# A long convolution and a cosine-gated layer: the last transform step with its data as weights, and x turned in blocks

## The chip, the cores and the metric

The kernel runs on one core of one Trainium2 chip, in one launch, in float32 throughout. The core has a matrix engine (TensorE, here PE, with PEld for its weight loads), a vector engine (DVE), a scalar engine (ACT), GpSimd (POOL), and SyncE (SP), which here does nothing but issue DMAs. The metric is the device time of one execution in microseconds; a kernel is judged by the median of its runs.

## What is computed

Four sequences of 12480 positions and 128 channels pass through a causal convolution and then through a layer with a cosine gate. Cut to what matters:

```python
h_filt = np.maximum(pos_emb @ w1, 0.0) @ w2 * window      # (12480, 128), one filter per channel
u = x * v                                                 # (4, 12480, 128)
y = irfft(rfft(u, 2 * S) * rfft(h_filt, 2 * S))[:, :S]    # convolution over the positions
tokens = (x * y).reshape(49920, 128)
h = tokens @ w_in                                         # 128 -> 2048
out = (h * np.cos(h)) @ w_out                             # 2048 -> 128
```

## The kernel before

The convolution is made as a Fourier transform of length 11520 = 96 x 120 that is written as matmuls. A position is a pair (n1, n2): n1 counts 104 rows of 120 positions, n2 the place in a row. For each of the four batches there are four steps, each a generator that emits its instructions a bit at a time.

- `f1_units`: 64 steps, one per pair of channels. `f1_mm` (L407) takes a slice of the buffer `slots` as weights (104 rows, 124 columns) against the table `c1`; ACT or DVE bring the result back into `slots` (`f1_evict`).
- `f2_units`: 48 steps, one per pair of frequencies. `f2_mm` (L448) has a table `w` as weights and moves `slots`; DVE and POOL multiply by the filter's transform `h` (L471 to L474).
- `i1_units`: 64 steps, one per pair of channels. `i1_mm` (L479) takes `slots` as weights (120 rows, 96 columns); ACT and DVE bring the result back (L487, L489).
- `i2_units`: 30 groups of four n2. `i2_mm` (L504) has a table `t` as weights (96 rows, 104 columns, from `tm`, which batch 0 makes and the others load from `td`) and moves 128 channels from `slots`; eight matmuls make one PSUM bank of 104 rows (n1) by 4 x 128. `i2_out` multiplies it by `xs`, the same rows of x, on DVE (L511) and stores the product `zs` in the DRAM buffer `zd`.

The one buffer `slots` has 128 partitions and, in each, 64 pairs of channels by 240 places by the 2 channels of a pair. So one channel over all places lies 8 bytes apart, and all channels of one place lie in pairs 1920 bytes apart. During `i2_units` of a batch, `u_units` of the next one loads x and v (L376), multiplies them (L395) and writes their sums into `slots` (L401).

The layers work in 97 tiles of up to 512 tokens: 4 n2 by up to 128 rows of `zd`. `moe_load` fetches a tile as `zb`, with the tokens on the partitions (L727); `moe_turn` turns it by four transposes on PE (L126 with `zb`) and a copy on ACT (L737), to have the channels on the partitions (`at`). Then come 16 steps: `moe_up` (L743, then ACT L746, DVE L749, POOL L752), `moe_act` (ACT L757, DVE L759) and, four steps later, `moe_down` (L768). `moe_back` turns the result by four more transposes (L126 with `ot`), and `moe_store` writes it out in one to three DMAs (L794).

The order is written out by hand and is the same on every run: each engine works through its own list in that order, and so does SyncE with its DMAs. The main loop goes through the layers' steps, and after each it lets the convolution's generators run for an amount of work that they state themselves:

```python
            owed += 1.0
            while owed > 0.0:
                owed -= next(conv, owed)
```

One group of `i2_units` counts 3.5 layer steps in batch 0, 3 in batches 1 and 2, and 1.5 in batch 3, which has no next batch beside it. `load(n)` first lets the convolution run until the rows of tile n have been made, so the layers start after the first group, and once batch 3 is through they are alone. In `i2_units` the loads for a group are issued one group ahead (`before`), in batch 3 two ahead.

Every DMA is issued by SyncE. The DMAs take eight semaphores in turn, so each waits until the one eight places before it has landed.

Of the kernel before, what the change touches and what calls it, by code (L numbers as in the profile page):

```python
# [30 lines left out]
def kernel(  # L31
# [74 lines left out]
    LAG = 4  # L106
    WCOL = 256

    dram = ctx.enter_context(tc.tile_pool(name="dram", bufs=1, space=DRAM))
    hd = dram.tile([N1 // 2, N2, 2, CB, 4], F32, name="hd")  # L110
    zd = dram.tile([NROWS, G, D], F32, name="zd")
# [241 lines left out]
    def filter_out(pool, bank, aT, slots, j, w2_sb):  # L353

        ps = bank()
        for i, jj in enumerate((j, H - 1 - j)):
            nc.tensor.matmul(ps[0:FR, i * 2 * D:(i + 1) * 2 * D], aT[:, jj, 0:FR],
                             w2_sb[:, :], start=True, stop=True)
        above = pool.tile([FR, 2, CB, 2], F32, name="above", bufs=2)
        pj = ps[0:FR, :].rearrange("p (n b i) -> p n b i", n=4, i=2)  # L360
        nc.scalar.copy(out=above[:, :, :, :], in_=pj[:, 2:4])
        a = H - 2 - 2 * j
        for place, op in ((a, ALU.add), (ODD + a, ALU.subtract)):
            nc.vector.tensor_tensor(
                slots[0:FR, :, place:place + 2, :].transpose([0, 2, 1, 3]),
                pj[:, 1::-1], above[:, :, :, :], op=op)
# [14 lines left out]
    def clear_gap(u):  # L381

        nc.gpsimd.memset(u[:, :, H:ODD, :], 0.0)
# [13 lines left out]
    def u_sums(u, tiles, a):  # L397
        both = tiles[0][:, :, :].rearrange("p h (n b i) -> p h n b i", n=UA, i=2)
        below, above = both[:, 0, ::-1, :, :], both[:, 1, :, :, :]
        for place, op, e in ((a, ALU.add, nc.gpsimd), (ODD + a, ALU.subtract, nc.vector)):  # L400
            e.tensor_tensor(u[0:R, :, place:place + UA, :].transpose([0, 2, 1, 3]),  # L401
                            below, above, op=op)


    def f1_mm(ps, u, b, i):

        nc.tensor.matmul(ps[0:KE, i * 2 * N1:(i + 1) * 2 * N1], u[:, b, 0:KE, i],  # L407
                         c1[0:u.shape[0], :, :].rearrange("p r k -> p (r k)"),
                         start=True, stop=True)
# [10 lines left out]
    def f1_evict(ps, b, share):  # L420
        copy, negated = f1_takers(b, share)
        pj = ps[:, 0:4 * N1].rearrange("p (i r k) -> p r k i", i=2, r=2)
        copy(out=parts[0:ODD, :, :, b, :], in_=pj[0:ODD])
        yield
        copy(out=parts[ODD:KE, 0, :, b, :], in_=pj[ODD:KE, 1])
        negated(parts[ODD:KE, 1, :, b, :], pj[ODD:KE, 0])
        yield

    def f1_evict_filter(ps, b, share):

        copy, negated = f1_takers(b, share)
        pj = ps[:, 0:4 * N1].rearrange("p (i k) -> p k i", i=2)
        near, far = ftile[:, b, :, :], above[:, b, :, :]
        copy(out=near[0:ODD], in_=pj[0:ODD, 0:N1 + KF])
        copy(out=far[0:ODD], in_=pj[0:ODD, N1 + KF:])
        yield
        copy(out=near[ODD:KE, 0:N1], in_=pj[ODD:KE, N1:])
        negated(near[ODD:KE, N1:], pj[ODD:KE, 0:KF])
        negated(far[ODD:KE], pj[ODD:KE, KF:N1])
        yield  # L440

    def f2_mm(ps, w, k1, i, filt=False):


        k = k1 + i
        pi = ps[0:N2, :].rearrange("p (r b g i) -> p g r b i", r=2, g=2, i=2)[:, i]
        if not filt:
            nc.tensor.matmul(pi, w[:, i, :], parts[0:KE, :, k], start=True, stop=True)  # L448
        elif k < KF:
            both = ftile[0:KE, :, k:k + N1 + 1:N1, :].rearrange("p b r i -> p r b i")  # L450
            nc.tensor.matmul(pi, w[:, i, :], both, start=True, stop=True)
        else:
            for r, src in enumerate((ftile[0:KE, :, k, :], above[0:KE, :, k - KF, :])):
                nc.tensor.matmul(pi[:, r], w[:, i, :], src, start=True, stop=True)

    def f2_product(pool, ps, h, k1, whole):


        y = parts[0:N2, :, k1:k1 + 2, :, :].rearrange("p r k b i -> p r b (k i)")
        t = pool.tile([N2, 2, CB, 4], F32, name="t", bufs=1 + whole)  # L460
        uu = ps[0:N2, :].rearrange("p (r b j) -> p r b j", r=2, j=4)
        if whole:
            for r, (dst, hh) in enumerate(((y, h[:, :, :, :]), (t[:, :, :, :], h[:, ::-1, :, :]))):
                u = uu[:, r]
                twice = bass.AP(tensor=u.tensor, offset=u.offset,
                                ap=[u.ap[0], [0, 2], *u.ap[1:]])
                nc.vector.tensor_tensor(dst, twice, hh, op=ALU.mult)  # L467
                yield
# [8 lines left out]
    def i1_mm(ps, b, i):  # L477
        for r in range(2):
            nc.tensor.matmul(  # L479
                ps[0:N1, (i * 2 + r) * N2:(i * 2 + r + 1) * N2],  # L480
                parts[0:N2, r, :, b, i],
                cs[:, r, :], start=True, stop=True)

    def i1_evict(pool, ps, b):
# [3 lines left out]
        for h, op in ((0, ALU.add), (1, ALU.subtract)):  # L488
            nc.vector.tensor_tensor(slots[0:N1, b, h * N2:(h + 1) * N2, :], pj[:, 0],  # L489
                                    other[:, :, :], op=op)  # L490
            yield

    def i2_mm(ps, t, g, part):
        for i in range(part * G // 2, (part + 1) * G // 2):
# [8 lines left out]
            for r, place in enumerate(places):  # L503
                nc.tensor.matmul(ps[0:R, i * D:(i + 1) * D], t[:, i, r, :],  # L504
                                 slots[0:N1, :, place, :], start=(r == 0), stop=(r == 1))

    def i2_out(pool, ps, xs, b, g):
        if b == 0:
            yield
        zs = pool.tile([R, 2, UA, D], F32, name="zs")  # L510
        nc.vector.tensor_tensor(  # L511
            zs[:, :, :, :].rearrange("p h n d -> p (h n d)"), ps[0:R, :],
            xs[:, :, :].rearrange("p h n -> p (h n)"), op=ALU.mult)
        z = zs[:, :, :, :].rearrange("p h n d -> p (h n) d")
        row = (b * NG + g) * R
        if row > 0:
            nc.sync.dma_start(zd[row:row + R, :, :], z)
        else:
            zbs[0] = z
        made[0] += 1  # L520
        yield

    rows_psum = []
    made = [0]
    zbs = {}
# [65 lines left out]
    def f2_units(bank):  # L591
        with tc.tile_pool(name="there", bufs=3) as pool:
            ws, hs = {}, {}

            def before(j):
                ws[j] = pool.tile([KE, 2, N2], F32, name="w")
                nc.sync.dma_start(ws[j][:, :, :], wd[j, :, :, :])
                hs[j] = pool.tile([N2, 2, CB, 4], F32, name="h")
                nc.sync.dma_start(hs[j][:, :, :, :], hd[j, :, :, :, :])
# [10 lines left out]
    def f2_both_units(bank):  # L610

        with tc.tile_pool(name="both", bufs=2) as pool:
# [15 lines left out]
            def after(j, ps):  # L628
                h = pool.tile([N2, 2, CB, 4], F32, name="h", bufs=3)
                nc.scalar.activation(h[:, :, :, :].rearrange("p r b j -> p (r b j)"),  # L630
                                     ps[1][0:N2, :], AF.Copy, scale=1.0 / M)
                nc.sync.dma_start(hd[j, :, :, :, :], h[:, :, :, :])
# [32 lines left out]
    def i2_units(bank, b, bufs):  # L665

        with tc.tile_pool(name="back", bufs=2, side="left" if b else "right") as pool:
            ts, xss = {}, {}

            def before(j):  # L670
                ts[j] = pool.tile([N1, G, 2, R], F32, name="tm", bufs=bufs)
                xss[j] = pool.tile([R, 2, UA * D], F32, name="xs", bufs=bufs)
                load_pairs(xss[j], x, b, n2s(j)[0], n2s(j)[UA])
                if b == 0 and j not in SOME:
                    return make_group(pool, j, ts[j], 1)
                nc.sync.dma_start(ts[j][:, :, :, :], td[j, :, :, :, :])

            def mm(j, ps, i):
                if i == 0:
                    ps = bank()  # L680
                i2_mm(ps, ts[j], j, i)
# [3 lines left out]
                             lambda j, ps: i2_out(pool, ps, xss.pop(j), b, j),  # L685
                             4 if b == 0 else 2, ahead=bufs - 1, skip=int(b == 0))

    def inverse_units(bank, b):
# [6 lines left out]
        new = u_units(b + 1, 3, slots[0:R, :, :, :],  # L695
# [10 lines left out]
    def forward_units(bank, back):  # L706
# [3 lines left out]
        yield from f1_units(bank, slots[0:R, :, :, :])  # L710
# [13 lines left out]
    def moe_load(pool, n):  # L724
        m, row = rows_of(n), first_row(n)
        zb = pool.tile([P, G, D], F32, name="zb", bufs=2)
        nc.sync.dma_start(zb[0:m, :, :], zd[row:row + m, :, :])  # L727
        zbs[n] = zb

    def moe_turn(pool, n):  # L730
        m = rows_of(n)
        zb = zbs.pop(n)
        pt = ps_h.tile([P, BANK], F32, name="ph")
        for i in range(G):
            transpose(pt[:, i * m:(i + 1) * m], zb[0:m, i, :], ident)
        at = pool.tile([D, BANK], F32, name="at")
        nc.scalar.copy(out=at[:, 0:G * m], in_=pt[:, 0:G * m])  # L737
# [62 lines left out]
    with tc.manual_schedule():  # L800
        with tc.tile_pool(name="psum", bufs=8, space=PSUM) as psum, \
# [5 lines left out]
            slots = spool.tile([P, CB, 2 * N2, 2], F32, name="slots")  # L807
            parts = slots[:, :, 0:2 * N1, :].rearrange("p b (r k) i -> p r k b i", r=2)
            above = slots[:, :, 2 * N1:2 * N2, :]
            aT = above.rearrange("p b j i -> p b (j i)")  # L810
# [5 lines left out]
            with tc.tile_pool(name="layers", bufs=1, side="right") as pool:  # L816
# [10 lines left out]
                first_u = u_units(0, 3, slots[0:R, :, :, :],  # L827
# [24 lines left out]
            ftile = fpool.tile([P, CB, N1 + KF, 2], F32, name="ftile")  # L852
            clear_gap(ftile[0:FR, :, :, :])
# [5 lines left out]
            f1 = f1_units(bank, ftile[0:FR, :, :, :], 0.53, f1_evict_filter)  # L859
# [27 lines left out]
            beside(f1_units(bank, slots[0:R, :, :, :], 0.55),  # L887
# [32 lines left out]
        mpool = ctx.enter_context(tc.tile_pool(name="moe", bufs=2))  # L920

# [24 lines left out]
        moe_turn(mpool, 0)  # L946
        steps = [(n, c) for n in range(NALL) for c in range(NFC)]
        hidden, gates, ots, obs = {}, {}, {}, {}
        for i in range(len(steps) + LAG):
            if i < len(steps):  # L950
# [3 lines left out]
                if c == NFC - 4 and n + 2 < NALL:  # L954
                    load(n + 2)
# [8 lines left out]
            if i < len(steps):  # L964

                if c == (LAG - 1 if n else NFC - 2) and n + 1 < NALL:
                    moe_turn(mpool, n + 1)
# [37 lines left out]
```

## Time and profile before

| | us |
|---|---|
| median of 3 runs | 3762.23 |
| lowest and highest | 3761.11, 3762.27 |
| span of the profiled execution, first to last instruction | 3758.9 |
| PE busy in it | 3690.6 |
| DVE, POOL, ACT busy | 2773.7, 2557.6, 2508.2 |
| first to last L504 of batch 0 | 338 to 562 |
| of batch 1 | 1178 to 1385 |
| of batch 2 | 1992 to 2208 |
| of batch 3 | 2814 to 2948 |
| layers alone | 2948 to the end |

The profiled execution has no time of its own beside its span; the runs' median is 3.3 us above it. Of the profile the page gives busy times and the chain of waits, and the trace behind it the single instructions. A 32-bit matmul shows as two instructions on PE, a transpose as one. Busy time of PE counts from the start of an instruction to its modelled end, so instructions overlap and the duration in a row is longer than the distance from one start to the next. Where a row gives `96*104 96x128`, the weights have 96 rows and 104 columns and 128 columns are moved. The rows of SyncE (SPq) are the time that it takes to issue a DMA, not the transfer.

### The profile page before, as it was taken

What the parts mean: (1) busy time and instruction counts of PE and PEld (TensorE: products, weight loads), DVE (VectorE), ACT (ScalarE), POOL (GpSimd) and SP (SyncE); (2) the same over time, 40 slices, a digit from 0 to 9 for tenths busy, and PEclk for the clock granted to TensorE, in tenths of its full rate; (3) what the DMA queues carried; (4) which work ended last, traced back from release to release, by engine and by line L of the source; (5) the groups of instructions that cost most, each with busy time, mean ns of one, the idle gap of its engine ahead of it and who ended that gap; (6) DMA issues with size and microseconds to landing.
All of it is one profiled execution on the core that took longest, in us unless ns stands there. A gap on an engine that the chain in (4) does not pass through costs nothing.

```text
span 3758.9 us, 47177 instructions
## 1 busy us (share of the span) xinstructions
PE 3690.6 (98%) x13546; PEld 2110.4 (56%) x13546; DVE 2773.7 (74%) x5586; ACT 2508.2 (67%) x4660; POOL 2557.6 (68%) x2318
## 2 busy tenths in 40 slices
PE   7898999999999999999999999999999999999999
PEld 6777555555566556555565556555566544444444
DVE  8887997687866787788766776788765666666666
ACT  5757776766665557766665567666664677777777
POOL 6666776588845665688745664788644677777776
PEclk9999999999999999999999999999999999999999
DMA  6263551022203650122104530122105200000000
GB/s 167 64 185 107 155 167 33 25 72 79 72 12 91 181 151 12 40 79 77 52 18 128 180 105 21 52 79 76 38 21 172 76 23 17 17 23 18 17 23 13
DMA packets 209499, 276.14 MB, mean 73 GB/s; under 512 B 17111, under 2 KB 146535, under 8 KB 209111
## 3 DMA queue, kind: packets, MB, share of 16 engines
q1 hardware_dynamic: 209239, 273.12, 24.8%
q8 instruction: 109, 1.79, 0.2%
q14 instruction: 151, 1.24, 0.1%
HBM read 193.64 MB, written 79.42 MB: 73 GB/s over the span
## 4 chain that ended last, share of the span: by engine, by line
PE 88%; DVE 3%; POOL 3%; ACT 2%; DMA 2%; issue 1%; SPq 0%; POOLq 0%; DVEq 0%; ACTq 0%
PE ph L743 33%; PE acc L768 28%; PE cv L504 5%; PE cv L768 5%; PE cv L479 4%; PE cv L407 3%; PE cv L448 3%; PE ph L126 2%; POOL f L752 1%; PE ps L407 1%; PE ps L448 1%; DMA tm<-td 1%; DMA wd<-w 1%; ACT cs L757 1%; DVE k L749 1%
## 5 line engine op out<-in xcount | busy, mean ns | idle before, releaser
L752 POOL TENSOR_TENSOR f<-a,k 128x512 f32<-128x512 f32 (+1 forms) x1568 | 1986.2, 1267 | 1060.5 <-DVE k L749 1059.1
L743 PE MATMUL ph<-at,w_in_sb 128*128 128x512 f32 (+1 forms) x3136 | 1599.0, 591 | 3.7 <-DVE gt L759 2.7
L746 ACT ACTIVATE a<-ph,quarter 128x512 f32<-128x512 f32 (+1 forms) x1568 | 1071.2, 683 | 704.8 <-PE ph L743 695.2
L768 PE MATMUL acc<-gt,w_out_sb 128*128 128x512 f32 (+1 forms) x2688 | 1370.3, 591 | 0.0
L759 DVE TENSOR_TENSOR gt<-ph,cs 128x512 f32<-128x512 f32 (+1 forms) x1568 | 1077.3, 687 | 359.9 <-ACT cs L757 341.8
L757 ACT ACTIVATE cs<-f 128x512 f32<-128x512 f32 (+1 forms) x1568 | 981.0, 626 | 366.6 <-POOL f L752 364.3
L749 DVE TENSOR_SCALAR k<-a 128x512 f32<-128x512 f32 (+1 forms) x1568 | 792.9, 506 | 550.7 <-ACT a L746 524.2
L768 PEld LDWEIGHTS acc<-gt,w_out_sb 128*128 128x128 f32 x2688 | 508.4, 189 | 642.8 <-issue 631.9
L743 PEld LDWEIGHTS ph<-at,w_in_sb 128*128 128x128 f32 x3136 | 553.2, 190 | 337.7 <-issue 257.5
L474 POOL TENSOR_TENSOR slots<-slots,t 120x256 f32<-120x256 f32 x384 | 312.9, 821 | 59.9 <-DVE t L467 25.6
L504 PEld LDWEIGHTS cv<-slots,tm 96*104 96x104 f32 x1920 | 238.6, 169 | 106.8 <-issue 85.4
L504 PE MATMUL cv<-slots,tm 96*104 96x128 f32 x1920 | 251.7, 273 | 9.9 <-POOL tm L297 5.0
L768 PE MATMUL cv<-gt,w_out_sb 128*128 128x512 f32 (+1 forms) x448 | 224.5, 583 | 1.0 <-DVE gt L759 1.0
L479 PEld LDWEIGHTS cv<-cs,slots 120*96 120x96 f32 x1536 | 176.7, 167 | 67.2 <-issue 65.2
L479 PE MATMUL cv<-cs,slots 120*96 120x120 f32 x1536 | 183.2, 266 | 0.0
L448 PEld LDWEIGHTS cv<-slots,w 124*120 124x120 f32 x576 | 103.7, 184 | 124.3 <-issue 112.3
L407 PEld LDWEIGHTS cv<-c,slots 104*124 104x124 f32 x768 | 132.6, 192 | 72.2 <-issue 60.0
L448 PE MATMUL cv<-slots,w 124*120 124x256 f32 x576 | 173.0, 380 | 0.0
L407 PE MATMUL cv<-c,slots 104*124 104x192 f32 x768 | 151.8, 327 | 5.4 <-DVE gt L759 3.5
L768 PEld LDWEIGHTS cv<-gt,w_out_sb 128*128 128x128 f32 x448 | 84.9, 190 | 104.8 <-issue 99.5
L489 DVE TENSOR_TENSOR slots<-cv,other 96x240 f32<-96x240 f32 x384 | 133.1, 394 | 1.5 <-ACT other L487 1.4
L395 DVE TENSOR_TENSOR xt<-xt,vt 104x256 f32<-104x256 f32 x177 | 132.6, 751 | 0.6 <-DMA vt<-in_v_dram 0.6
(131 smaller groups left out, 2520.9 us busy)
## 6 DMA issues: line engine op xcount, KB each, us to landing
h<-hd SPq DMA_DIRECT2D x144, 240.0 KB
tm<-td SPq DMA_DIRECT2D x96, 312.0 KB
xt<-in_x_dram SPq DMA_DIRECT2D x120, 208.0 KB
vt<-in_v_dram SPq DMA_DIRECT2D x120, 208.0 KB
xs<-in_x_dram SPq DMA_DIRECT2D x120, 208.0 KB
zd<-zs SPq DMA_DIRECT2D x119, 208.0 KB
zb<-zd SPq DMA_DIRECT2D x96, 256.0 KB
w<-wd SPq DMA_DIRECT2D x144, 116.2 KB
```

The lines of the kernel that those rows point to most:

```text
L407: nc.tensor.matmul(ps[0:KE, i * 2 * N1:(i + 1) * 2 * N1], u[:, b, 0:KE, i], c1[0:u.shape[0], :, :].rearrange("p r k -> p (r k)"), start=Tr ...
L448: nc.tensor.matmul(pi, w[:, i, :], parts[0:KE, :, k], start=True, stop=True)
L474: nc.gpsimd.tensor_tensor(y[:, r], y[:, r], t[:, r], op=op)
L479: nc.tensor.matmul(ps[0:N1, (i * 2 + r) * N2:(i * 2 + r + 1) * N2], parts[0:N2, r, :, b, i], cs[:, r, :], start=True, stop=True)
L504: nc.tensor.matmul(ps[0:R, i * D:(i + 1) * D], t[:, i, r, :], slots[0:N1, :, place, :], start=(r == 0), stop=(r == 1))
L743: nc.tensor.matmul(ph[:, 0:m], w_in_sb[:, c * P:(c + 1) * P], ats[n][:, 0:m], start=True, stop=True)
L746: nc.scalar.activation(a[:, 0:m], ph[:, 0:m], AF.Identity, bias=quarter[:, 0:1], scale=INV_TWO_PI)
L749: nc.vector.tensor_scalar(out=k[:, 0:m], in0=a[:, 0:m], scalar1=ROUND, scalar2=ROUND, op0=ALU.add, op1=ALU.subtract)
L752: nc.gpsimd.tensor_tensor(f[:, 0:m], a[:, 0:m], k[:, 0:m], op=ALU.subtract)
L757: nc.scalar.activation(cs[:, 0:m], f[:, 0:m], AF.Sin, scale=TWO_PI)
L759: nc.vector.tensor_tensor(gt[:, 0:m], ph[:, 0:m], cs[:, 0:m], op=ALU.mult)
L768: nc.tensor.matmul(accs[n][:, 0:m], w_out_sb[:, c, :], gt[:, 0:m], start=(c == 0), stop=(c == NFC - 1))
```

## The change

Four things go together.

1. `slots` is laid out as 240 places by 128 channels, with the channels innermost; so are `ftile`, `hd` and `h`. The slices that L407 and L479 take as weights now have their elements 512 bytes apart, and the evictions of these two steps write pairs of channels 512 bytes apart. What L448 moves, what the products of the second step read and write, and the batch sums become contiguous.
2. In the last step the roles are exchanged: `slots` at one place is the weights (96 rows, 128 columns) and `t` moves (104 columns). The result has the channels on the partitions: 128 by 4 x 104. It is stored so in `zd`, and `moe_load` fetches a tile straight into `at`, in two or three DMAs of pieces of 32 to 416 bytes; `moe_turn` is gone with its transposes and copies. The first group's product is the first tile's `at` itself. `load(n + 1)` is called at step 2 of tile n, where `load(n + 2)` was called at step 12.
3. x has to be turned too, for the product in `i2_out`. `blocks_load` fetches it, for each of the 4 n2 and each 32 channels of 128, in a DMA of its own: 8 partitions by 13 pieces of 32 channels (128 bytes). So 16 DMAs make a tile `xb` of 128 partitions by 13 by 32.
4. `blocks_turn` turns each 32 x 32 block of it by one DVE transpose of 128 x 416 into `xt`. `xb` has three buffers; its loads are issued one group further ahead than before.

In the lists of the engines 392 PE transposes and 97 ACT copies are gone, 120 DVE transposes have come, 120 loads of `xs` have become 1920 of `xb`, and 97 loads of `zb` have become 217 of `at`.

```diff
-            slots = spool.tile([P, CB, 2 * N2, 2], F32, name="slots")
+            slots = spool.tile([P, 2 * N2, D], F32, name="slots")
...
     def f1_mm(ps, u, b, i):
-        nc.tensor.matmul(ps[0:KE, i * 2 * N1:(i + 1) * 2 * N1], u[:, b, 0:KE, i],
+        nc.tensor.matmul(ps[0:KE, i * 2 * N1:(i + 1) * 2 * N1], u[:, 0:KE, 2 * b + i],
...
     def i1_mm(ps, b, i):
-                parts[0:N2, r, :, b, i],
+                parts[0:N2, r, :, 2 * b + i],
...
             for r, place in enumerate(places):
-                nc.tensor.matmul(ps[0:R, i * D:(i + 1) * D], t[:, i, r, :],
-                                 slots[0:N1, :, place, :], start=(r == 0), stop=(r == 1))
+                nc.tensor.matmul(ps[0:D, i * R:(i + 1) * R], slots[0:N1, place, :],
+                                 t[:, i, r, :], start=(r == 0), stop=(r == 1))
+
+    def blocks_load(t, b, g):
+        for i, n2 in enumerate(n2s(g)):
+            for a in range(D // SQ):                     # SQ = 32, ROWB = 8, NB = 13
+                start = x[b, n2, a * SQ:(a + 1) * SQ]
+                first = a * SQ + i * ROWB
+                nc.sync.dma_start(
+                    t[first:first + ROWB, :, :],
+                    bass.AP(tensor=start.tensor, offset=start.offset,
+                            ap=[[N2 * D, ROWB], [ROWB * N2 * D, NB], [1, SQ]]))
+
+    def blocks_turn(pool, t):
+        xt = pool.tile([D, G, R], F32, name="xt", bufs=2)
+        nc.vector.transpose(
+            xt[:, :, :].rearrange("d i (n r) -> d n i r", r=ROWB),
+            t[:, :, :].rearrange("p n (i r) -> p n i r", r=ROWB))
+        return xt
...
-    def i2_out(pool, ps, xs, b, g):
+    def i2_out(pool, ps, xts, turn_next, b, g):
...
-            zs[:, :, :, :].rearrange("p h n d -> p (h n d)"), ps[0:R, :],
-            xs[:, :, :].rearrange("p h n -> p (h n)"), op=ALU.mult)
+            zs[:, 0:G * R], ps[0:D, 0:G * R],
+            xts.pop(g)[:, :, :].rearrange("d i n -> d (i n)"), op=ALU.mult)
...
+        turn_next(g + 1)
+        yield
...
     def moe_load(pool, n):
         m, row = rows_of(n), first_row(n)
-        zb = pool.tile([P, G, D], F32, name="zb", bufs=2)
-        nc.sync.dma_start(zb[0:m, :, :], zd[row:row + m, :, :])
-        zbs[n] = zb
-
-    def moe_turn(pool, n):
...
-        for i in range(G):
-            transpose(pt[:, i * m:(i + 1) * m], zb[0:m, i, :], ident)
         at = pool.tile([D, BANK], F32, name="at")
-        nc.scalar.copy(out=at[:, 0:G * m], in_=pt[:, 0:G * m])
+        to = at[:, 0:G * m].rearrange("d (i n) -> d i n", i=G)
+        done = 0
+        while done < m:
+            group, n1 = divmod(row + done, R)
+            rows = min(m - done, R - n1)
+            nc.sync.dma_start(to[:, :, done:done + rows], zd[group, :, :, n1:n1 + rows])
+            done += rows
         ats[n] = at
...
             def before(j):
...
-                load_pairs(xss[j], x, b, n2s(j)[0], n2s(j)[UA])
+                if j == 0:
+                    fetch(0)
+                fetch(j + 1)
...
-                if c == NFC - 4 and n + 2 < NALL:
-                    load(n + 2)
+                if c == 2 and 0 < n < NALL - 1:
+                    load(n + 1)
```

## The prediction

> **What bounds the kernel now.** I read the page first. Its first part and its chain of waits name one engine:
>
> ```profile
> PE 3690.6 (98%) x13546; PEld 2110.4 (56%) x13546; DVE 2773.7 (74%) x5586; ACT 2508.2 (67%) x4660; POOL 2557.6 (68%) x2318
> ...
> PE 88%; DVE 3%; POOL 3%; ACT 2%; DMA 2%; issue 1%; SPq 0%; POOLq 0%; DVEq 0%; ACTq 0%
> ```
>
> TensorE is the bound, so a matmul taken away is a gain wherever nothing else is nearly as late. The table by stages shows how near the rest is. The four stretches are the last transform steps (first to last L504) of batches 0 to 3; columns: window, length, then busy time of PE, PEld, DVE, ACT and POOL (instructions), clock, DMA share, GB/s.
>
> ```profile
> 338.00:562.00 224.00, 220.88 (x899) 129.96 (x900) 202.73 (x357) 163.93 (x328) 168.37 (x159) 0.99 0.54 165
> 1178.00:1385.00 207.00, 205.35 (x863) 120.69 (x862) 158.32 (x281) 114.03 (x187) 131.74 (x112) 1.00 0.59 175
> 1992.00:2208.00 216.00, 213.16 (x883) 124.15 (x882) 162.53 (x289) 119.74 (x196) 136.84 (x116) 1.00 0.57 169
> 2814.00:2948.00 134.00, 134.00 (x685) 88.95 (x684) 68.12 (x121) 59.76 (x100) 57.68 (x46) 1.00 0.56 166
> ```
>
> Each holds 30 groups: one group takes 7.5, 6.9, 7.2 and 4.5 us. In the chain of the last of them every step is PE: the first line is one group's 16 instructions, 1.78/16 = 0.111 us each, the second half a step of the layers.
>
> ```profile
> 2820.12 1.78 PE cv L504 x16
> 2821.89 0.86 PE ph L743 x2
> ```
>
> The table has no column for SyncE, so I read its timeline there (start, duration):
>
> ```profile
> 2830.56 0.33 SPq L376 DMA_DIRECT2D xs<-in_x_dram  x1
> 2830.98 0.35 SPq L676 DMA_DIRECT2D tm<-td  x1
> 2831.38 0.38 SPq L517 DMA_DIRECT2D zd<-zs  x1
> 2834.05 0.33 SPq L376 DMA_DIRECT2D xs<-in_x_dram  x1
> ```
>
> Issuing one DMA occupies the queue for 0.40 us from start to start, whatever its bytes; three make 1.25 us of a 4.5 us group. Last the rows by shape (mean ns behind the comma) and the source view of the output stores (shortest/median/longest ns):
>
> ```profile
> L504 PEld LDWEIGHTS cv<-slots,tm 96*104 96x104 f32 x1920 | 238.6, 169 | 106.8 <-issue 85.4 <-POOL tm L297 5.2 <-PE acc L768 5.1
> ...
> L126 PE MATMUL ph<-ident,zb 128*128 128x128 f32 x384 | 57.7, 273 | 0.0
> ...
> L407 PEld LDWEIGHTS cv<-c,slots 104*124 104x124 f32 x768 | 132.6, 192 | 72.2 <-issue 60.0 <-POOL slots L401 6.0 <-PE ph L743 3.8
> ...
> L749 DVE TENSOR_SCALAR k<-a 128x416 f32<-128x416 f32 x16 | 7.5, 471 | 6.1 <-ACT a L746 5.1 <-ACT cs L757 1.0
> ```
>
> ```profile
> L794 SPq DMA_DIRECT2D out_dram<-ob x209: 282/367/1363, 398.7 to 3755.5; - x105
> ```
>
> Matmul durations overlap, so I cost PE by starts in the trace: 429 ns from one 512-column instruction to the next, 109 for a transpose of 128 columns, 111 for L504, 102 for L479, 162 for L407.
>
> **Part by part: TensorE.** All 392 transposes into the layers go: four per tile of 0.109 us, 0.44 us for each of 97 tiles, 42 us in all. About 20.6 tiles lie in the four stretches (105, 90, 90 and 46 steps of 16); where those get another bound the saving is lost, so 76 x 0.44 = 33 us count. The 97 copies on ACT behind them (0.574 us) were off the path.
>
> In the last step data and table change sides: 128 weight columns and 104 moving instead of 104 and 128. By streaming, 104 columns need 104 x 0.83 + 3 = 89 ns, 42 us less over 1920 instructions. But loads of 128 columns start no closer than 108 ns anywhere in the trace (104 columns: 88; 96: 85), and one load must end for each matmul. So 108 against 111: 4 to 6 us, between ends of 0 and 42, and nothing inside a stretch with another bound. The second step's moving operand becomes contiguous: L448 goes from 223 and 218 ns to the 216 of the contiguous L357, about 4 us. Credit: 37 us.
>
> **Strides.** The weights of L407 and L479 were read 8 bytes apart and will be 512 apart; no row shows that stride. At 8 bytes 96 columns cost 167 ns, contiguous (L357) 163. Below, the price is nothing: L407 has 162 ns for a load of 108, L479 102 for 85. Above, I take a doubled load: L479 170 for 102, 68 x 2048 = 139 us; L407 216 for 162, 54 x 1280 = 69 us; together 208. I take nothing, by the 8-byte row as the nearest, and keep 208 for the range. [...] Evictions in pairs 512 bytes apart: DVE writes pairs 1920 bytes apart in 416 ns (L401, third stretch) and contiguous 256 in 412 (L473), so nothing; on ACT they are off the path.
>
> **VectorE.** 120 transposes of 128x416, not in the trace: between 0.47 us (L749 row above) and 1.2 us (twice the 0.586 of a two-input 128x416). I take 0.6, as one input and one pass resemble the first. Less 0.09 for the narrower product, 30 x 0.5 = 15 us per stretch; idle DVE time there is 21, 49, 53 and 66 us, which covers it. In the first stretch at 1.2 us it would not (33 over 21), 12 us more.
>
> **SyncE and the DMAs.** One load of x per group becomes sixteen of 8 partitions in 128-byte pieces: 1920 issues for 120. I price one from stores of 8 partitions: 0.282 us alone (shortest of L794) plus 0.03 between instructions, 0.31 at best; directly behind another DMA eight of them took 0.297 to 0.373 (middle 0.36), plus 0.05: 0.35 to 0.42. They stand sixteen in a row, so I take 0.41. Other issues per group: table 0.40, store 0.42, the layers' loads (now 217 in pieces, for 97) and output stores 0.2 in the last stretch and 0.4 elsewhere, and before the last the next batch's x and v, 0.8. So 16 x 0.41 + 1.0 = 7.6 us of queue per group in the last stretch, where PE needs 4.5; 6.6 + 2.0 = 8.6 in the others, where it needs 7.5, 6.9 and 7.2.
>
> The wait this adds sits on VectorE: the transpose of group j waits for its sixteen loads. Behind it in DVE's order stand the layers' L749 and L759; POOL and ACT wait for these, and PE for L759's product after four steps. So PE goes at SyncE's pace. Three block buffers hold two groups (three in the last batch) loaded beforehand; that shortens the stretch once. Stretches by queue, with the last groups' own work behind (4 to 5 us):
> batch 3: 27 x 7.6 + 4 = 208, for 134: +74;
> batch 1: 28 x 8.6 + 5 = 245, for 207: +38; batch 2, for 216: +29; batch 0, for 224: +21.
> Sum +162. Nothing later gives it back, since PE is the bound again in the next stage.
>
> The layers' own load moves from step 12 of the tile two before to step 2 of the tile before. It still has 14 steps of 1.72 us, 24 us, for a landing of 3 to 4 us; uncovered it would cost these 3 to 4 us per tile. The batch sums of POOL and DVE write contiguously (L401 on POOL 0.906 us, contiguous L395 0.812): off the path, nothing.
>
> Bytes: 1664 pieces per group. In the trace a packet of 4 bytes takes 9 ns, 256 bytes 18, 1024 bytes 46; at 14 ns the blocks fill 23 us of engine time per group. The 8-partition store raises its semaphore 9 times, a 128-partition one 16, so I take eight engines: 2.9 us each, besides about 3.5 for the group's other traffic, inside 8.6. Issue comes first, but not by far. [...] Every DMA also waits for the one eight places earlier, whose semaphore it reuses; at 3 us to land, 3/8 = 0.38 us hides under 0.41.
>
> **Sum.** The span is 3758.9 us, the median of the runs 3762.2, so 3.3 lie outside. 3762.2 - 37 + 162 = 3887 us.
>
> **Rivals.**
> - *The queue keeps up* (faster). At 0.31 us per issue the last stretch is 27 x 6.0 + 4 = 166, +32, and the others stay with PE (28 x 7.0 + 5 = 201); credit 41 + 8: 3745. With the last stretch hidden too, 3712. It decides below 0.33 us, where +42 meets the credit. For it: the shortest stores. Against: all eight behind another DMA were above 0.34.
> - *Transfers land late*: 4.8 us to land, through eight places 0.6 us each. 27 x 10.6 + 4 = 290 (+156), 28 x 11.6 + 5 = 330 (+106, +123, +114): 499 - 37, 4224. For it: loads landed after up to 6.9 us. Against: the median is 2.8 to 3.7.
> - *Strided weights load slowly*: up to 208 on top, 4095; at one and a half times only L479 pays, 26 x 2048 = 53, 3940.
>
> **How the numbers follow.** The queue bound (issues of 0.36 to 0.50 us, 3800 to 4050) gets 0.62, the queue keeping up 0.15, late transfers 0.10, slow weights 0.09, a draw between credit and queue 0.04. Under 3740 lies about half of the second, over 4080 most of the third and part of the fourth: the range is 3740 to 4080. A measurement of this kernel can tell 0.2%, 7.5 us, from no change: faster 0.15, same 0.03, slower 0.82.
>
> **What would show it.** Right: the batch 3 stretch grows to about 208 us with PE well under full; SyncE issues without a pause there, start to start about 0.41 us; DVE's transpose waits on the block loads; the stage after it is 0.44 us shorter per tile. Wrong: stretches no longer than before with SyncE idle in them (the queue keeps up); SyncE waiting between blocks (late transfers); L479 starts more than 110 ns apart (slow weights); the new L504 at 89 ns (load does not bind).

## The result and the profile after

| | us |
|---|---|
| median before, 4 runs beside the changed kernel | 3761.71 |
| median after, 4 runs | 4148.59 (4146.33 to 4151.21) |
| ratio | 1.103, 95% interval 1.101 to 1.104 |
| span of the profiled execution after | 4146.5 |
| forecast | 3887, range 3740 to 4080 |

The change makes the kernel 387 us slower. The direction was foreseen, the size was not: the time lies above the range. First the page's busy times and its chain of waits:

```profile
PE 3923.2 (95%) x13154; PEld 2316.2 (56%) x13154; DVE 2805.1 (68%) x5706; ACT 2468.0 (60%) x4562; POOL 2544.9 (61%) x2318
...
PE 77%; DMA 10%; POOL 4%; DVE 3%; SPq 3%; issue 2%; ACT 2%; DVEq 0%; POOLq 0%; ACTq 0%
```

PE executes 392 instructions fewer and is busy 233 us longer, and still its share falls from 98% to 95%. So there are two losses: work on PE has become longer, and PE waits. The waits fall into four places. The windows from the first to the last instruction of the last step (now L507) of batches 0 to 3 (window, length, then busy time of PE, PEld, DVE, ACT and POOL with instructions, clock, DMA share, GB/s):

```profile
371.20:648.70 277.50, 239.26 (x887) 138.90 (x888) 205.27 (x392) 164.16 (x324) 169.68 (x160) 0.91 0.51 132
1294.60:1571.40 276.80, 234.03 (x852) 132.42 (x851) 167.56 (x315) 115.91 (x189) 130.49 (x116) 0.92 0.53 130
2215.10:2496.80 281.70, 235.47 (x852) 133.93 (x851) 169.00 (x317) 115.83 (x189) 131.71 (x116) 0.90 0.53 128
3140.70:3354.30 213.60, 164.78 (x668) 103.34 (x667) 78.49 (x150) 58.25 (x96) 56.93 (x46) 0.85 0.44 104
```

Counted in the same way they took 227, 206, 214 and 131 us before (the tables ahead of the result, with rounded window ends, gave 224, 207, 216 and 134): +51, +71, +67 and +83, in all +272 us. The remaining +116 lies elsewhere: +33 before the first of them, +33, +35 and +36 between them (where `f1`, `f2` and `i1` of the next batch run), -21 in the layers' tail. The rows of the two steps that read `slots` as weights name that second part. L479 before, then the same two steps after (L407's row before stands in the prediction):

```profile
L479 PEld LDWEIGHTS cv<-cs,slots 120*96 120x96 f32 x1536 | 176.7, 167 | 67.2 <-issue 65.2 <-PE ph L743 1.9
```

```profile
L482 PEld LDWEIGHTS cv<-cs,slots 120*96 120x96 f32 x1536 | 276.5, 255 | 60.3 <-issue 59.6 <-PE ph L778 0.7
...
L409 PEld LDWEIGHTS cv<-c,slots 104*124 104x124 f32 x768 | 186.5, 299 | 62.0 <-issue 28.1 <-POOL slots L404 6.8 <-PE ph L778 5.8
```

So the loads take 255 and 299 ns where they took 167 and 192. From the start of one matmul to the next, middle values in the trace, `i1` (L482, before L479) goes from 102 to 165 ns, `f1` (L409, before L407) from 162 to 212. What PE and DVE wait for, from the list of waits (total us, times, longest):

```profile
PE cv L507 <- DMA tm<-td: 159.7, 63, 7.2
DVE zs L535 <- DMA zd<-zs: 108.7, 25, 6.3
...
PEld cv L507 <- DMA tm<-td: 57.7, 20, 5.5
```

and SyncE's timeline in the last stretch (start, duration, with runs of one form on one line):

```profile
3200.42 0.35 SPq L541 DMA_DIRECT2D zd<-zs  x1
3200.87 0.82 SPq L829 DMA_DIRECT2D out_dram<-ob  x2
3201.79 0.37 SPq L708 DMA_DIRECT2D tm<-td  x1
3202.26 6.57 SPq L516 DMA_DIRECT2D xb<-in_x_dram  x16
3208.88 0.35 SPq L541 DMA_DIRECT2D zd<-zs  x1
3209.32 0.37 SPq L708 DMA_DIRECT2D tm<-td  x1
```

SyncE goes from one table load to the next in 7.53 us, with gaps of 0.1 us between the rows; before, a group of that stretch took 4.5 us in all. The table's load stands behind sixteen blocks and a store, and PE waits for it.

### The profile page after: what moved, and what is told of

It reads as the page before. It is cut to its first block, busy times and chain, and to the rows that moved or that the text cites. A ratio compares the mean times of both kernels' runs of the same rounds, so it can differ in the third digit from the quotient of the medians.

```text
span 4146.5 us, 48727 instructions
## 1 busy us (share of the span) xinstructions
PE 3923.2 (95%) x13154; PEld 2316.2 (56%) x13154; DVE 2805.1 (68%) x5706; ACT 2468.0 (60%) x4562; POOL 2544.9 (61%) x2318
## 4 chain that ended last, share of the span: by engine, by line
PE 77%; DMA 10%; POOL 4%; DVE 3%; SPq 3%; issue 2%; ACT 2%; DVEq 0%; POOLq 0%; ACTq 0%
PE ph L778 28%; PE acc L803 23%; PE cv L482 6%; DMA tm<-td 6%; PE cv L803 4%; PE cv L507 4%; PE cv L409 4%; PE cv L451 3%; POOL f L787 2%; PE ps L482 2%; PE ps L409 2%; SPq L516 2%; DMA xb<-in_x_dram 2%; DMA hd<-h 2%; PE ph L130 1%
## 5 line engine op out<-in xcount | busy, mean ns | idle before, releaser
L778 PE MATMUL ph<-at,w_in_sb 128*128 128x512 f32 (+1 forms) x3136 | 1637.8, 604 | 5.4 <-DVE gt L794 5.1
L803 PE MATMUL acc<-gt,w_out_sb 128*128 128x512 f32 (+1 forms) x2688 | 1400.3, 603 | 5.9 <-ACT ot L809 5.8
L778 PEld LDWEIGHTS ph<-at,w_in_sb 128*128 128x128 f32 x3136 | 569.6, 195 | 364.8 <-issue 294.3
L507 PEld LDWEIGHTS cv<-tm,slots 96*128 96x128 f32 x1920 | 276.6, 214 | 306.4 <-issue 178.3
L507 PE MATMUL cv<-tm,slots 96*128 96x104 f32 x1920 | 285.0, 298 | 170.3 <-DMA tm<-td 159.7
L482 PEld LDWEIGHTS cv<-cs,slots 120*96 120x96 f32 x1536 | 276.5, 255 | 60.3 <-issue 59.6
L482 PE MATMUL cv<-cs,slots 120*96 120x120 f32 x1536 | 269.9, 322 | 0.0
L409 PEld LDWEIGHTS cv<-c,slots 104*124 104x124 f32 x768 | 186.5, 299 | 62.0 <-issue 28.1
L409 PE MATMUL cv<-c,slots 104*124 104x192 f32 x768 | 182.9, 368 | 4.5 <-DVE gt L794 4.4
L535 DVE TENSOR_TENSOR zs<-cv,xt 128x416 f32<-128x416 f32 x119 | 69.3, 582 | 117.4 <-DMA zd<-zs 108.7
```

The lines of the kernel that those rows point to most:

```text
L482: nc.tensor.matmul(ps[0:N1, (i * 2 + r) * N2:(i * 2 + r + 1) * N2], parts[0:N2, r, :, 2 * b + i], cs[:, r, :], start=True, stop=True)
L507: nc.tensor.matmul(ps[0:D, i * R:(i + 1) * R], slots[0:N1, place, :], t[:, i, r, :], start=(r == 0), stop=(r == 1))
L778: nc.tensor.matmul(ph[:, 0:m], w_in_sb[:, c * P:(c + 1) * P], ats[n][:, 0:m], start=True, stop=True)
L803: nc.tensor.matmul(accs[n][:, 0:m], w_out_sb[:, c, :], gt[:, 0:m], start=(c == 0), stop=(c == NFC - 1))
```

## Experiments

Two theories stood against each other at the start. One: the strided weights cost what the prediction had as its upper bound, and the list of 16 loads costs the rest, the two independent of each other. The other: one cause makes both, for instance the many small transfers, which disturb PE's reading as well as the lists.

**The layout alone.** The kernel before, with `slots`, `ftile`, `hd` and `h` channels innermost; loads, transposes and roles as before.

```diff
-            slots = spool.tile([P, CB, 2 * N2, 2], F32, name="slots")
+            slots = spool.tile([P, D // Q, 2 * N2, Q], F32, name="slots")     # Q = 128
```

> The kernel before with the new buffer layout alone (channels innermost, weight columns of f1 and i1 512 bytes apart); loads, transposes, roles of the last step and the vector work stay as before. Theory (the stride alone makes the weight loads slow, whatever the rest): i1 starts every 165 ns in place of 102 (2,048 of them, +129 us) and f1 every 213 in place of 162 (1,280, +65), less some 4 us for the f2 products, so 3762 + 190 = 3950 us, with the stretches of the last step as before (224, 201, 209 and 129 us). Rival (the loads are slow only beside the changed kernel's many small transfers): 102 and 162 ns stay, 3755 to 3765 us.

Measured: 3904.96 us, 3901 to 3909 (ratio 1.038, 1.036 to 1.039), +142. By starts `i1` has 165 to 166 ns and `f1` 212 to 213, and the loads are as long as in the changed kernel:

```profile
L484 PEld LDWEIGHTS cv<-cs,slots 120*96 120x96 f32 x1536 | 276.1, 255 | 57.3 <-issue 55.4 <-PE ph L749 1.9
...
L411 PEld LDWEIGHTS cv<-c,slots 104*124 104x124 f32 x768 | 185.2, 300 | 57.4 <-issue 27.8 <-POOL slots L405 6.0 <-PE ph L749 3.8
```

The four stretches take 229, 207, 217 and 130 us, as before; of the rise 30 us lie before the first and 37, 38 and 39 between them. So the stride alone makes the loads slow; the small transfers have no part in it. The time is 45 us under what was expected. The gross price, 63 ns x 2048 + 51 x 1280 = 194 us, is paid in the three later batches for the most part (45 of gross each, 38 measured), but at the start only half (58 and 30): there `f1` stood 198 to 203 ns apart in the mean before already, since PE waited for ACT and DVE, and is at 216 to 219 now.

**How far apart.** The same kernel with four and with eight channels innermost (Q = 4 and 8: columns 16 and 32 bytes apart), and the changed kernel with one unused element behind each place (516 bytes; two small buffers of the filter's stage have one copy fewer there, and the filter's own buffer keeps 512):

```diff
-            slots = spool.tile([P, 2 * N2, D], F32, name="slots")
+            wide = spool.tile([P, 2 * N2, D + 1], F32, name="slots")
+            slots = wide[:, :, 0:D]
```

> The kernel before with four channels innermost in the buffer in place of two: weight columns of f1 and i1 16 bytes apart in place of 8; nothing else is changed. Theory (what costs is that two neighbouring columns no longer lie within the same 16 bytes): the whole price is there already, 165 and 213 ns, some 3950 us. Rival (what costs is the large stride, a multiple of 512 bytes): 102 and 162 ns stay, 3762 us within 10.

> The kernel before with eight channels innermost: weight columns 32 bytes apart. Theory (no two columns within 16 bytes is all that counts): i1 165 to 177 ns and f1 213 to 227, as at 16 and 512 bytes, 3900 to 3945 us. Rival (the price falls or rises with the distance): i1 clearly outside 160 to 180 ns.

> The changed kernel with one unused element after each place, so that columns lie 516 bytes apart in place of 512; the filter's own buffer keeps 512, and two small buffers of the filter's stage have one copy fewer. Rival (a multiple of 512 bytes costs): i1 falls from 165 to about 102 ns (2,048, -129 us) and f1 from 213 to 162 for 1,024 of 1,280 (-52 us), 4148 - 181 = 3967 us. [...]

| bytes between columns | kernel | time, us | `i1`, ns | `f1`, ns |
|---|---|---|---|---|
| 8 | before | 3762 | 102 | 162 |
| 16 | lay16 | 3940 | 176 | 226 |
| 32 | lay32 (one run) | 3951 | 179 | 231 |
| 512 | lay512 | 3905 | 165 | 212 |
| 512 | after | 4149 | 165 | 211 |
| 516 | pitch516 | 4179 | 174 | 223 |

In time: lay16 1.048 of before (1.046 to 1.049), pitch516 1.111 (1.109 to 1.113) where the changed kernel has 1.103. The whole price is there at 16 bytes, and it is not a matter of multiples of 512: with one element of padding the loads are slightly slower still (174 and 223 ns where the changed kernel has 165 and 211, and 4179 us where the rival had 3967). lay32 too lies just above its expectation (179 ns for 165 to 177). At 16 to 516 bytes a column costs 1.7 to 1.9 ns (165 ns for 96 columns, 231 for 124). At 8 bytes the loads stay within 102 and 162 ns, the pace of the 120 and 192 moving columns (0.85 ns each); what a load alone costs there was not seen. No distance between 8 and 16 bytes was tried. Why 512 is a little cheaper than 16, 32 or 516 stays open.

**One load.** The changed kernel with one x load a group, of the same bytes but not of the elements that the blocks need:

```diff
-        for i, n2 in enumerate(n2s(g)):
-            for a in range(D // SQ):
-                ...
+        start = x[b, g * UA, 0:SQ]
+        nc.sync.dma_start(t[:, :, :], bass.AP(tensor=start.tensor, offset=start.offset,
+                                              ap=[[D, P], [P * D, NB], [1, SQ]]))
```

> The changed kernel with one x load a group in place of 16: the same bytes in the same 128-byte pieces to the same tile, but not the elements that the blocks need, so the product with x is of other numbers. Theory (the length of SyncE's list is what holds the last step): the waits of PE for the t table and of VectorE for the layers' store go, the stretches of the last step come back to about those of before (224, 201, 209, 129), 4148 - 268 = 3880 us, up to 3920. Rival (the small pieces on the DMA engines, or the last step's own work, hold it): stretches near 274, 273, 275, 208 stay, 4100 us or more.

Measured: 3873.79 us, 3871 to 3878 (ratio 1.030, 1.028 to 1.031), 275 us below the changed kernel. Its stretches are back at those of before, and PE has no gap in three of them:

```profile
368.70:599.70 231.00, 226.14 (x887) 133.88 (x888) 209.36 (x390) 162.32 (x323) 171.94 (x160) 0.97 0.65 159
1246.90:1453.90 207.00, 207.00 (x853) 122.23 (x852) 166.05 (x315) 115.79 (x188) 131.05 (x115) 1.00 0.75 172
2097.60:2304.60 207.00, 207.00 (x852) 122.20 (x851) 166.05 (x314) 115.72 (x189) 130.89 (x115) 1.00 0.75 173
2948.60:3079.00 130.40, 130.40 (x669) 88.16 (x667) 79.23 (x148) 57.30 (x96) 56.27 (x46) 1.00 0.69 169
```

With this the change is taken apart, in one order of its parts: layout +142 (lay512 against before), exchanged roles without the transposes -31 (one_load against lay512), sixteen loads for one +275 (after against one_load); the sum is +386 of the 387 measured.

**Eight loads, and sixteen in large pieces.** Is it the number of issues, or what they carry? Both kernels again leave out which elements the blocks need. The first issues 8 loads of 16 partitions in the same 128-byte pieces, the second 16 loads of 8 partitions in pieces of 1664 bytes:

```diff
-                    ap=[[N2 * D, ROWB], [ROWB * N2 * D, NB], [1, SQ]]))      # 16 of these
+                    ap=[[D, 16], [P * D, NB], [1, SQ]]))                     # dose8: 8 of these
+                    ap=[[NB * SQ, 8], [1, NB * SQ]]))                        # big16: 16 of these
```

> The changed kernel with 8 x loads a group in place of 16: the same bytes in the same 128-byte pieces, not the elements that the blocks need, so the product with x is of other numbers. Theory (SyncE's list holds the last step only while it is longer than PE's work on a group): 8 issues of 0.36 us leave about 2.9 us less than 16 do, so a group's list of some 5 us is under the 6.9 us of the first three batches and near the 4.3 us of the last: 3874 to 3910 us. Rival (each load costs alike): 3874 + 275 x 7 / 15 = 4002 us.

> The changed kernel with its 16 x loads a group, each of 8 partitions, but in pieces of 1664 bytes in place of 128 (8 pieces a load in place of 104, the same bytes), not the elements that the blocks need, so the product with x is of other numbers. Theory (the number of issues is what fills SyncE's list, and the pieces do not matter): the stretches stay near 278, 277, 282 and 214 us, 4100 to 4150 us. Rival (the small pieces make the loads land late, and the list waits for their places): the waits between blocks go and the price falls from 0.47 to 0.36 us a block, 27 x 16 x 0.11 = 48 us a stretch, 3960 to 4000 us.

Measured: dose8 3914.85 us (3911 to 3915, ratio 1.041, 1.039 to 1.042), big16 4102.24 us (4100 to 4104, ratio 1.091, 1.089 to 1.092). Halving the issues takes 234 of the 275 us away; thirteen times fewer pieces take 46. A price per load, the same for each, is excluded (4002 was its value). In the first three stretches of dose8 (240, 210 and 214 us) the list is no longer than PE's work or hardly so (3910 us at most was expected); SyncE stands still for 38 us in the first of them before the loads of x and v. Only in the last, where PE has least to do, does the list still set the end (152 us for 130, and PE not full):

```profile
2964.40:3116.70 152.30, 138.24 (x669) 90.27 (x667) 79.96 (x149) 57.57 (x96) 56.36 (x46) 0.97 0.62 145
```

SyncE's list in the second stretch, start to start, shows what a block costs:

| second stretch | after | big16 |
|---|---|---|
| blocks issued | 432 | 432 |
| issuing them, us | 136.2 | 130.1 |
| between them (0.044 each at least), us | 65.6 | 64.0 |
| a block in all, us | 0.467 | 0.449 |
| the other 137 issues, us | 73 | 74 |

One issue has 0.315 us in the middle, 0.044 stand between two, and the other 0.11 us per block is waiting. It is mostly for a place among the eight semaphores, and not behind other blocks: in the list of waits of the changed kernel the block loads wait 66.3 us for `tm<-td` and 37.1 for `vt`, 6.6 for other blocks. These large loads take over 3 us to land (the table 4.3, `x` and `v` 3.4, where a block takes 1.8; middle values in the trace); eight blocks at 0.36 us are 2.9. This fits big16, which keeps the waits; what it gains is the issue, 0.293 us for 0.315, 42 us over 1920.

**Half of the blocks from GpSimd.** What is computed stays:

```diff
-                nc.sync.dma_start(
+                (nc.gpsimd if a % 2 else nc.sync).dma_start(
```

> The changed kernel, with every second block load issued from GpSimd in place of SyncE; what is computed stays. Theory (SyncE's list alone holds the last step): near the kernel with 8 loads a group, 3880 to 3940 us, if GpSimd, 61% busy, has room for 960 issues at SyncE's own 0.36 us (346 us in its span, 70%). Rival (the issue from GpSimd costs it over 1 us each, or it stands in its order and waits there): GpSimd is late for the layers and the time stays over 4050 us.

Measured: 4315.29 us (4313 to 4318, ratio 1.147, 1.146 to 1.149), slower than with one queue. An issue from GpSimd takes 618 ns of its time:

```profile
L516 POOL DMA_DIRECT2D xb<-in_x_dram x960 | 590.6, 618 | 62.9 <-DVE xt L524 47.2 <-issue 13.4 <-DVE k L784 2.3
```

The theory of this run failed, and the second half of the rival came: 618 ns are nearly twice SyncE's 315, though under 1 us, and they stand in the order of an engine on which the layers depend: `ACT cs` waits 1091 us for POOL's `f` where it waited 453, and the chain of waits has POOL at 16%. Whether a second queue helps on an engine with more room was not tried.

**The gain without its price.** What the change was able to gain are the 392 transposes. The exchanged roles with the pairs' layout, where the 128 channels of a place lie in pairs 1920 bytes apart, were not tried. But the transposes can go without the exchanged roles: before's layout and last step stay, and VectorE turns the product `zs` instead of x, in blocks of 32, from which four stores put it into `zd` with the channels outside.

```diff
+        zt = mpools[0].tile([P, G, D // SQ, SQ], F32, name="zt", bufs=2)
+        nc.vector.transpose(zt[:, :, :, :].rearrange("p i a n -> p (i a n)"), zs[:, :])
+        for n1 in range(0, R, SQ):
+            n = min(SQ, R - n1)
+            nc.sync.dma_start(
+                zd[b * NG + g, :, :, n1:n1 + n].rearrange("(a c) i n -> c i a n", c=SQ),
+                zt[n1:n1 + SQ, :, :, 0:n])
```

> The kernel before (its layout of two channels innermost, its last step with one x load a group), but the 392 transposes of the layers' inputs go another way: VectorE turns the product in blocks of 32 and four stores a group put the blocks into the layers' order. Theory (the roles' credit is what was foreseen, the stride and the list of 16 loads took it back): 392 x 0.109 = 42 us of PE and 392/4 copies of ScalarE go, 120 VectorE transposes of 0.6 us lie beside PE, three more SyncE issues a group fit into its list: 3762 - 42 + 5 for the first input's way through memory = 3725 us, 3715 to 3740. Rival (the four stores in 128-byte pieces come late for the layers' loads, or VectorE becomes late): 3770 us or more.

Measured: 3764.00 us (3759 to 3767, ratio 1.0006, 0.9997 to 1.0015): no change, where 3715 to 3740 was expected. The stretches had grown by 14, 11, 4 and 2 us. Its waits say where: PE waited for the table (first line), whose load stood in SyncE's list behind the stores and a load of x, which waited for VectorE, and for the first input's way through `zd` (second line):

```profile
PE cv L505 <- DMA tm<-td: 18.9, 24, 2.8
PE ph L741 <- issue: 8.1, 1, 8.1
```

So a second version changes only the order:

```diff
+        flush()                                  # the stores of the group before
         zs = zss[(b * NG + g) % 2]
...
+        late.append((b * NG + g, zt))            # stored one group later
...
+                nc.sync.dma_start(ts[j][:, :, :, :], td[j, :, :, :, :])
                 load_pairs(xss[j], x, b, n2s(j)[0], n2s(j)[UA])
-                nc.sync.dma_start(ts[j][:, :, :, :], td[j, :, :, :, :])
...
         load(0)
+        for _ in range(4):
+            next(conv)
```

> The kernel with VectorE's turn of the product, with three moves of order: the t table's load stands ahead of the x load, a group's four stores are issued one group later, behind the next table load, and four more steps of the convolution are issued before the layers begin. Theory (its PE waited for the t table behind stores that waited for VectorE, about 9 to 17 us in each of the second and third batch, and 8 us for the first input): these waits go, 3764 - 30 = 3734 us, 3725 to 3745. Rival (the credit is lost to the element engines or to the clock, not to these waits): 3755 us or more.

Measured: 3735.52 us (3733 to 3738, ratio 0.9934, 0.9920 to 0.9947). It beats both kernels, 26 us below the one before. The wait of PE for the table has fallen to

```profile
PE cv L505 <- DMA tm<-td: 3.4, 3, 1.8
```

and the stretches are at 230, 207, 210 and 132 us; the stages between them are 4 to 7 us shorter each and the tail 10. Of the 42 us that the transposes held, about 16 are still not seen. The trace has them, counted from each PE instruction's start to the next over the whole run: the last step takes 226 us for 218, `moe_up` 1350 for 1344 and `moe_back`'s transposes 47 for 43. What holds these up was not tried.

## Why the prediction failed, step by step

**The credit** came out near its number, partly by luck. The sum had 37 us: 33 for the transposes outside the four stretches and 4 for the second step's products. With the queue out of the way (one_load against lay512) all transposes could be had, and -31 was measured (the two profiled executions differ by 36). In these, counted from start to start, the transposes did take 45 us with them, but `moe_up` takes 12 us more, `moe_back` 2 more and `moe_down` 5 less. The second step takes 228 us before, 226 in lay512 and 228 in one_load, so its 4 us did not come. The exchanged matmul stands 112 ns apart in the middle, not 89, in line with a bound by its load, as foreseen; but 108 was counted, and over 1920 instructions it gains nothing (214 us in one_load, 215 in lay512). (The 108 was read too strictly: 30 of some 6300 loads of 128 columns start 57 to 107 ns apart in the trace before.) Of the 21 us by which the tail is shorter, 12 are its 108 transposes; the other 9 are 20 layer matmuls of 0.429 us that now run earlier.

**The strides are the first step that failed.** The prediction measured 102 and 162 ns at 8 bytes, took that as the nearest row to 512 and put the price at nothing. The upper bound in the same paragraph, 170 and 216 ns from a load whose doubling was the author's estimate, was within 5 ns of what came: 165 and 212. So the price was in the text and was only chosen against; on the path it is 142 us, because the start hides half of its share and the later batches a sixth. The reason given for the choice, the row at 8 bytes as the nearest, did not hold: lay16, at 16 bytes, has the whole price (176 and 226 ns), so a large distance is not what costs. At the four distances from 16 to 516 bytes a load of weights was measured at 1.7 to 1.9 ns a column. The rival "slow weights" deserved far more than 0.09.

**SyncE's list is the second, by its size.** The mechanism was right: in the stretches PE goes at the pace of the list. The stretch of batch 3 was forecast at 208 us and took 214, its group at 7.6 us and takes 7.5 in the lines above. The other three were forecast at 245 and took 277, 277 and 282. Two terms were short there. A block was priced at 0.41 us with the waits for the semaphores' places hidden, and costs 0.467: the issue itself is cheaper (0.36 from start to start), but the places are held by the large loads of the table, x and v, which land later than the 3 us assumed. The trace before had this already: there the table takes 3.7 us to land and the next batch's x 4.1, in the middle, where the prediction read 2.8 to 3.7 for all loads. And the rest of the list has 2.7 us a group (73 / 27) where 2.0 were counted. Of the difference about 0.2 is longer issues (an `at` load of 128 partitions in four pieces occupies SyncE for 0.52 to 0.63 us, not 0.40) and 0.5 is waiting for other engines, which was put at nothing. So 27 x (16 x 0.467 + 2.7) = 275 us. The sum of the four is +272 where +162 stood.

**The place of the wait was wrong**, without a price: the prediction had VectorE's transpose wait for its blocks. It waits 5.3 us in all:

```profile
L524 DVE STREAM_TRANSPOSE xt<-xb 128x416 f32<-128x416 f32 x120 | 72.1, 601 | 5.3 <-DMA xb<-in_x_dram 5.1
```

The blocks are issued two groups ahead, the table's load in batches 0 to 2 only one, and the store of `zs` follows the blocks of a later group. The list is late as a whole, and what is waited for is what has the least lead in it: PE waits 159.7 us for the table and VectorE 108.7 for the store, but 5.1 for the blocks. That the lead decides is read from the order of the list; no run moved the table's load alone in the changed kernel. The 601 ns of this row are the 0.6 us that the prediction took between 0.47 and 1.2.

**The rivals.** "The queue keeps up" needed less than 0.33 us for an issue; 0.36 is near to that, but the waits came on top. "Transfers land late" has a grain of truth in the semaphores' places, though not for the blocks. "Strided weights load slowly", with 208 us on top of the queue, gave 4095 us and was the nearest of all to 4149: 66 us too much for the stride (208 for 142), 113 too little for the list (162 for 275). The range ended 15 us below it. Either error alone would have left the time inside the range: 4149 - 142 = 4007, and 4149 - 113 = 4036.

## What to carry to other kernels

When a layout is turned round for one reader, list every instruction that reads the buffer as weights and look at how far apart its columns will lie: here weights with columns 8 bytes apart took 102 and 162 ns from start to start, 16 to 516 bytes apart 165 to 179 and 211 to 231, and the bound worked out from a doubled load was the better guess than the row of a smaller stride. A load split into many must be held against PE's time per group, with all other issues of the same queue in the sum, and here eight loads, with a list longer than PE's work only in the last stretch, cost 41 us of the 275. And a gain can be bought from an engine with room: the same transposes went from PE for 26 us of gain once VectorE turned the product and the stores stood behind the loads that PE needs.

## What was not expected of the hardware

The granted clock of PE fell where PE waited: 0.91, 0.92, 0.90 and 0.85 in the four stretches of the changed kernel, 0.97 and three times 1.00 in one_load. In the second stretch PE was busy 234 us for 852 instructions, against 207 us for 853. These 27 us did not set the end there, since PE stood idle for 43 us besides; whether they cost anything was not tried. The issue of a load by SyncE depended on its shape more than on its bytes: 0.329 us for the 208 KB of the next batch's x, 0.315 for a block's 13 KB; by shape 0.293 us for 8 partitions of one piece each (big16), 0.315 for 8 of thirteen, 0.439 for 16 of thirteen (dose8), 0.52 to 0.63 for 128 of four. A packet of 128 bytes took 13 ns, where the prediction took 14.
